# A first unit written out in one order, with unsplit second weights and more idle products

## The chip, the cores and the metric

The kernel runs on one core of a Trainium2 chip. The metric is the device time of one execution in microseconds (us): 1182.4 us, the median of 3 runs of the kernel before (1181.29 to 1183.06). A difference under 0.2% (2.4 us) cannot be told from no change here.

## The reference

Three blocks follow one another, on 8 batches. All inputs are random; the weights arrive as 8-byte floats and are rounded to 4-byte floats on the chip.

```python
# block 1: 8 batches, 8 heads, 512 tokens and 32 states of 64 numbers
scores = 1/8 * x @ state.T;  a  = softmax(scores)      # tokens read the states
scores2 = 1/8 * state @ x.T; a2 = softmax(scores2)     # states read the tokens
y = concat([a @ state, a2 @ x])                        # (8, 544, 512)
# block 2
xn = (y - mean) / sqrt(var + 1e-6) * g_ln
x2 = y + relu(xn @ w_ch1) @ w_ch2                      # w_ch1 512x2048, w_ch2 2048x512
# block 3
h = relu(x2 @ w_in);  c = conv over 3 neighbouring tokens of h
out = (h * sigmoid(c)) @ w_out                         # w_in 512x1024, w_out 1024x512
```

## The kernel before

**Units.** Block 2 is worked in nine units: units 0 to 7 are the 512 tokens of a batch, unit 8 (`NB`) the 256 state rows of all batches. In a unit the 2048 hidden numbers come in 16 pieces (m = 0 to 15) of 128. `L1(u, m)` makes piece m in a PSUM bank (`ph`), `relu_parts` brings it to SBUF, and `L2(u, m)` multiplies it with rows m of the second weights and adds into four PSUM banks (`acc`). `L1(u, m+1)` is always issued before `L2(u, m)`.

**Split numbers.** A 4-byte number is split into a rounded high part and the rest (`hH` and `hL`; weights `w[:, 0]` and `w[:, 1]`), both of the kind fp32r. `three` (lines 618 to 621) makes a product out of three matmuls: high by high, high by rest, rest by high. A product of two unsplit fp32 tiles (`L609`, `L647`) is one matmul of the program, and the trace shows two for it.

**Block 1 beside block 2.** While unit u is multiplied, generators (`token_norm(u)`, `attend(u+1)`) issue the norm of this batch and the attention of the next in small steps, one at each `gap(m)`. The tokens are not read out before `L1`: `z_tiles` multiplies the states of a batch with a quarter j of the first weights (`Z[u, j]`), and `L1` multiplies the attention weights (`AH`, `AL`) with that.

**Weights.** `Converter` rounds a raw 8-byte piece in steps: `round_1` (two ScalarE operations, L199, L200), `round_2` (two VectorE operations, L205, L206, and a GpSimd addition, L207), and for the second weights `third` (ScalarE L239, GpSimd L240), the split. There are 32 pieces: 16 of the first and 16 of the second weights. `z_first(j)` is unit 0's own step: it takes four rounded pieces of the first weights, makes their mean over the rows (L609), scales and shifts them on VectorE (L612), multiplies (L585), and stores them in DRAM (`w1d`, L615), from which all later units read them back through a ring of seven tiles (`pass_pairs`, L574). All DMAs are issued by SP, in order.

**What sets the order.** The first steps are written out by the string `START` (line 98, walked at line 777). From line 784 to the beginning of unit 1 a scheduler with a timeline of its own arranges the instructions (`need(2, m)` asks four pieces ahead; `tc.high_priority` in `gap`); from unit 1 on the order is as written. `warm` (line 766) issues products of a tile of zeros into a bank that nobody reads: 8 at the start and 2 in `START`.

**Names and lines.** PE is TensorE, DVE VectorE, ACT ScalarE, POOL GpSimd, SP SyncE. L361 reads tokens from states, L799, L290, L300, L325 are the states' attention of batch 0, L814 turns the convolution weights, L670 and L672 are `residual`.

Of the kernel before, what the change touches and what calls it, by code (L numbers as in the profile page):

```python
# [17 lines left out]
P = 128  # L18
# [24 lines left out]
def kernel(  # L43
# [29 lines left out]
    hH = new("hH", [2, S], F32R)  # L73
    hL = new("hL", [2, S], F32R)
# [14 lines left out]

    work = {**{c: f"b{c}" for c in "PQRUV"}, "s": "0"}  # L90
# [5 lines left out]

    WARM = 8
    START = "s0w1ws0a1bab01ca01cabcabc"
# [502 lines left out]
    def z_first(j):  # L601


        for q in range(KC):
            need(1, KC * j + q)
# [4 lines left out]
        for q in range(KC):  # L610
            t = w[q // 2][:, q % 2]
            V.scalar_tensor_tensor(t, t, gcol[:, q : q + 1], vp, op0=ALU.mult, op1=ALU.subtract)  # L612
        z_tiles(0, j, w)
        for g in range(2):
            nc.sync.dma_start(w1d[j, g], flat(w[g]))  # L615

# [11 lines left out]
    def hidden(m):  # L628
        return hH[:, m % 2], hL[:, m % 2]

    def relu_parts(m, p):
        h, l = (t[:, : p.shape[1]] for t in hidden(m))
        A.activation(h, p, AF.Relu)  # L633
        V.scalar_tensor_tensor(l, p, 0.0, f32(h), op0=ALU.max, op1=ALU.subtract)  # L634

    def L1(u, m):
# [13 lines left out]
        relu_parts(m, p)  # L650

    def L2(u, m, n):
        h, l = (t[:, :n] for t in hidden(m))
        for d in range(KC):
            c = slice(P * d, P * d + P)
            three(acc[d][:, :n], w2[m][:, 0, c], w2[m][:, 1, c], h, l, m == 0, m == M1 - 1)

    def residual(u, n):
# [10 lines left out]
        for d in range(KC):  # L669
            V.tensor_tensor(t[d], acc[d], rstd[u], op=ALU.mult)  # L670
        for d in range(KC):
# [4 lines left out]
    w2 = {}  # L676
# [13 lines left out]
    AHEAD = 4  # L690

    def need(a, m):
        i = place_of[a, m]
        conv_a.ensure(min(i + AHEAD, conv_a.total - 1))
        return conv_a.done[i]

# [8 lines left out]
    def whole(i):  # L705

        a, m = order[i]
        if a == 2:
            return None
        if m % 2 == 0:  # L710
            rounded.append(new(f"r{RAWS + m // 2 % 2}", [2, S]))
        if m + RAWS < M1:
            load_weight(place_of[1, m + RAWS])
# [7 lines left out]
    V.memset(f32(hL), 0.0)  # L721
# [44 lines left out]
    def warm(n):  # L766
        for _ in range(n):
            T.matmul(acc[3], hL[:, 1, :P], hL[:, 0], start=True, stop=True)

    warm(WARM)  # L770
    steps = {
        "s": state_start(),
        "0": tokens_start(0, x0T[0], sets[0]),
        "1": tokens_start(1, x0T[1], sets[1]),
    }
    conv_steps = {"a": conv_a.first, "b": conv_a.second, "c": conv_a.third}
    for c in START:
        if c == "w":
            warm(1)
        elif c in steps:  # L780
            next(steps[c], None)
        else:
            conv_steps[c]()
    tc_start.close()
    load_state(1)
    banks["free"] = pat

    round_1(craw, c0)
    round_2(craw, c0)

    def states_start():
        starts = [work, {"V": spare[5], "R": spare[6], "s": "1"}]
        E2Ts, z2s = [], []
        for g in range(2):
# [8 lines left out]
            E2 = new(starts[g]["R"], [S])  # L803
            z2s.append(state_weights(sc, E2, starts[g]))
            E2Ts.append(state_weights_t(E2, starts[g]))
        yield
        srs = [state_read(0, g, E2Ts[g]) for g in range(2)]
        srzs = [state_scale(g, srs[g], z2s[g], starts[g]) for g in range(2)]
        yield
        for g in range(2):  # L810
            state_store(0, g, srzs[g])
        yield
        cp = bank()
        T.transpose(cp[:, :24], c0[:, 0], ident[:24, :24])  # L814
        A.activation(cw, cp[:, :24], AF.Copy)

# [54 lines left out]
    units = [*range(NB - 1), NB, NB - 1]  # L871
    LAST = units[-1]
    for u, follow in zip(units, [*units[1:], None]):
# [11 lines left out]
        if u == 0:  # L885
            made += [(2, z_first, 1), (6, z_first, 2), (10, z_first, 3), (13, z_step, 1, 0)]
        elif u < NB:
            made += [(0, z_step, u, 1), (3, z_step, u, 2), (7, z_step, u, 3)]
            if u != LAST:
                made.append((10, z_step, LAST if follow == NB else follow, 0))  # L890

        def gap(m):
            if made and m >= made[0][0] and banks["held"] is None:
                _, make, *which = made.pop(0)
                make(*which)
            elif u == 0:
                with tc.high_priority(offset=100):
                    next(tasks, None)
# [196 lines left out]
```

## Time and profile before

| | |
|---|---|
| median of three runs | 1182.4 us |
| the profiled execution / its span | 1177.81 us / 1176.0 us |
| PE busy | 1125.9 us (96%) |
| DVE busy | 726.6 us (62%) |
| ACT / POOL busy | 444.2 / 207.8 us |
| chain that ended last: PE / DVE / ACT | 80% / 12% / 3% |
| granted PE clock, mean | 0.981 |
| read-back of first weights (`r<-w1d`): issue to landing | 4.5 us |

The span is what the trace shows between the first and the last instruction; the execution's own time has 1.8 us around it. A busy PE is not a PE at its peak: a matmul of 512 columns shows some 0.39 us of its own, but in a stream the next starts earlier, so the distance from start to start is the price of one.

### The profile page before, as it was taken

What the parts mean: (1) busy time and instruction counts of PE and PEld (TensorE: products, weight loads), DVE (VectorE), ACT (ScalarE), POOL (GpSimd) and SP (SyncE); (2) the same over time, 40 slices, a digit from 0 to 9 for tenths busy, and PEclk for the clock granted to TensorE, in tenths of its full rate; (3) what the DMA queues carried; (4) which work ended last, traced back from release to release, by engine and by line L of the source; (5) the groups of instructions that cost most, each with busy time, mean ns of one, the idle gap of its engine ahead of it and who ended that gap; (6) DMA issues with size and microseconds to landing.
All of it is one profiled execution on the core that took longest, in us unless ns stands there. A gap on an engine that the chain in (4) does not pass through costs nothing.

```text
span 1176.0 us, 14628 instructions
## 1 busy us (share of the span) xinstructions
PE 1125.9 (96%) x5459; PEld 863.8 (73%) x5459; DVE 726.6 (62%) x1134; ACT 444.2 (38%) x788; POOL 207.8 (18%) x314
## 2 busy tenths in 40 slices
PE   5698899999999999999989999999999999999997
PEld 4365567777777777777767888788788888888885
DVE  4899666566566475565665622577677666666553
ACT  5665333323233233233233222565344434334332
POOL 2565400000000000000000000265433312213110
PEclk8699999999999999999999999999999999999999
DMA  9643533432243333334314124322112102100001
GB/s 298 206 171 108 158 96 105 108 95 90 72 109 85 81 111 76 78 120 108 95 56 107 38 101 155 119 72 90 37 54 72 37 37 80 37 36 36 1 37 45
DMA packets 129283, 106.31 MB, mean 90 GB/s; under 512 B 103332, under 2 KB 107452, under 8 KB 128188
## 3 DMA queue, kind: packets, MB, share of 16 engines
q1 hardware_dynamic: 129212, 105.37, 29.6%
q8 instruction: 43, 0.70, 0.2%
q14 instruction: 28, 0.23, 0.1%
HBM read 83.85 MB, written 21.50 MB: 90 GB/s over the span
## 4 chain that ended last, share of the span: by engine, by line
PE 80%; DVE 12%; ACT 3%; issue 2%; POOL 2%; SPq 0%; DMA 0%; ACTq 0%; DVEq 0%; POOLq 0%
PE acc L619 14%; PE acc L620 14%; PE acc L621 14%; PE ph L619 7%; PE ph L620 7%; PE ph L621 7%; PE pat L585 2%; PE pat L621 2%; PE pat L619 2%; PE pat L620 2%; PE pat L361 2%; PE ph L647 2%; DVE tn L500 1%; ACT bQ L488 1%; DVE ctmp L206 1%
## 5 line engine op out<-in xcount | busy, mean ns | idle before, releaser
L619 PE MATMUL acc<-hH,w 128*128 128x512 f32 (+1 forms) x576 | 221.6, 395 | 2.2 <-ACT hH L633 2.2
L620 PE MATMUL acc<-hL,w 128*128 128x512 f32 (+1 forms) x576 | 220.4, 383 | 1.8 <-DVE hL L634 1.7
L621 PE MATMUL acc<-hH,w 128*128 128x512 f32 (+1 forms) x576 | 220.1, 382 | 0.0
L634 DVE SCALAR_TENSOR_TENSOR hL<-ph,hH 128x512 fp32r<-128x512 f32 (+1 forms) x144 | 94.2, 657 | 183.4 <-ACT hH L633 183.2
L633 ACT ACTIVATE hH<-ph 128x512 fp32r<-128x512 f32 (+1 forms) x144 | 81.6, 569 | 208.9 <-PE ph L621 171.3
L619 PEld LDWEIGHTS acc<-hH,w 128*128 128x128 f32 x576 | 108.1, 188 | 54.5 <-issue 15.9
L1008 DVE SCALAR_TENSOR_TENSOR w<-w,cw,w 128x544 f32<-128x544 f32 x128 | 109.9, 860 | 38.0 <-POOL w L1006 36.2
L620 PEld LDWEIGHTS acc<-hL,w 128*128 128x128 f32 x576 | 109.2, 190 | 24.3 <-DVE hL L634 4.2
L621 PEld LDWEIGHTS acc<-hH,w 128*128 128x128 f32 x576 | 109.0, 189 | 21.7
L207 POOL TENSOR_TENSOR ctmp<-ctmp,AH 128x512 int32<-128x512 int32 x1 | 1.3, 1304 | 610.7 <-DVE ctmp L206 610.7
L619 PE MATMUL ph<-AH,ZH 128*128 128x512 f32 x256 | 104.3, 408 | 0.7 <-ACT ZH L594 0.7
L620 PE MATMUL ph<-AL,ZH 128*128 128x512 f32 x256 | 100.9, 394 | 0.0
L621 PE MATMUL ph<-AH,ZL 128*128 128x512 f32 x256 | 100.1, 395 | 0.0
L989 ACT ACTIVATE w<-w 128x544 f32<-128x544 f32 x64 | 42.1, 657 | 129.4 <-DVE w L1008 129.4
L996 DVE TENSOR_TENSOR w<-w,w 128x512 fp32r<-128x512 f32 x64 | 49.5, 774 | 42.9 <-ACT w L995 42.1
L990 DVE TENSOR_TENSOR w<-w,w 128x544 f32<-128x544 f32 x64 | 48.8, 762 | 39.5 <-ACT w L989 39.5
L619 PEld LDWEIGHTS ph<-AH,ZH 128*128 128x128 f32 x256 | 48.5, 190 | 19.5 <-issue 6.6
L995 ACT ACTIVATE w<-w 128x512 fp32r<-128x512 f32 x64 | 40.4, 631 | 52.4 <-DVE w L990 47.4
L1006 POOL TENSOR_SCALAR w<-w,cw 128x544 f32<-128x544 f32 x64 | 47.7, 746 | 61.8 <-ACT w L1002 58.4
L621 PEld LDWEIGHTS ph<-AH,ZL 128*128 128x128 f32 x256 | 48.2, 189 | 11.8 <-issue 0.8
L620 PEld LDWEIGHTS ph<-AL,ZH 128*128 128x128 f32 x256 | 48.6, 190 | 9.7
L997 POOL COPY w<-w 128x32 f32<-128x32 f32 x64 | 17.5, 273 | 177.5 <-DVE w L990 177.5
(439 smaller groups left out, 2182.0 us busy)
## 6 DMA issues: line engine op xcount, KB each, us to landing
r<-w1d SPq DMA_DIRECT2D x64, 512.0 KB, 4.5
out_dram<-w SPq DMA_DIRECT2D x34, 256.0 KB, 2.2
w<-in_moe_w_ch_dram SPq DMA_DIRECT2D x16, 512.0 KB, 8.0
r<-in_moe_w_ch_dram SPq DMA_DIRECT2D x16, 512.0 KB, 4.9
x2d<-XT SPq DMA_DIRECT2D x8, 1024.0 KB, 4.9
bP<-in_x_dram SPq DMA_DIRECT2D x112, 64.0 KB, 2.5
bP<-in_x_dram SPq DMA_DIRECT2D x28, 256.0 KB, 3.8
w1d<-r SPq DMA_DIRECT2D x8, 512.0 KB, 2.6
```

The costliest lines, as they stand in the source:

```text
L361: T.matmul(xr[ql], s[:, 2 * g + ql], a, start=i == 0, stop=i == 2)
L619: T.matmul(o, lh, rh, start=first, stop=False)
L620: T.matmul(o, lh, rl, start=False, stop=False)
L621: T.matmul(o, ll, rh, start=False, stop=last)
L633: A.activation(h, p, AF.Relu)
L634: V.scalar_tensor_tensor(l, p, 0.0, f32(h), op0=ALU.max, op1=ALU.subtract)
L989: A.activation(c, c, AF.Sigmoid)
L990: V.tensor_tensor(c, c, h[:, 1 : SEQ + 1], op=ALU.mult)
L995: A.activation(g[:, 0], c[:, :S], AF.Copy)
L996: V.tensor_tensor(g[:, 1], c[:, :S], f32(g[:, 0]), op=ALU.subtract)
L1006: G.tensor_scalar(c, h[:, 0:SEQ], cw[:, f : f + 1], 0.0, op0=ALU.mult, op1=ALU.add)
L1008: V.scalar_tensor_tensor(c, h[:, k : k + SEQ], cw[:, k * FF + f : k * FF + f + 1], c, op0=ALU.mult, op1=ALU.add,)
```

## The change

Unit 0 is no longer arranged by the scheduler. Fourteen generators, one letter each, are stepped in the order of a string of 196 letters, up to the last step of unit 0. The second weights stay whole in unit 0: `L2(0, m)` multiplies the unsplit hidden piece with an unsplit weight, and `relu_parts` leaves the rest out there. The split of a second weight (now ACT L674 and DVE L675, none on POOL) comes later: six at the end of unit 0 (`SPLITS`), ten in unit 1 (behind `L2(1, 4)` to `L2(1, 13)`). Whole weights lie in pairs, and splits go to other places (`slot2`). The `w` letters stand for 24 zero products; the two of the old string are gone, the eight at the start stay. `residual` and `z_first` may stop halfway.

```diff
-    START = "s0w1ws0a1bab01ca01cabcabc"
+    START = "ss01abaa0b101aawwwwwwwwwwww0bwwww1SabaSbwwwwzbaLLzPbSawwwwPNSN..."
+    SPLITS = 6
...
     def relu_parts(u, m, p):
+        if u == 0:
+            A.activation(hid["H"][:, m % 2], p, AF.Relu)
+            return
+        if (u, m) == (1, 0):
+            hid["H"] = new("hH", [2, S], F32R)
...
     def L2(u, m, n):
...
-            three(acc[d][:, :n], w2[m][:, 0, c], w2[m][:, 1, c], h, l, m == 0, m == M1 - 1)
+            if u == 0:
+                T.matmul(acc[d], whole2[m][:, c], h, start=m == 0, stop=m == M1 - 1)
+            else:
+                three(acc[d][:, :n], w2[m][:, 0, c], w2[m][:, 1, c], h, l, m == 0, m == M1 - 1)
+
+    def split_w2(m):
+        w = w2[m] = new(slot2(m), [2, DM], F32R)
+        A.activation(w[:, 0], whole2[m], AF.Copy)
+        V.tensor_tensor(w[:, 1], whole2[m], f32(w[:, 0]), op=ALU.subtract)
...
+    streams = {
+        "s": (state_start(), acc),
+        "0": (tokens_start(0, x0T[0], sets[0]), acc),
+        "1": (tokens_start(1, x0T[1], sets[1]), acc),
+        "a": (firsts(), acc),
+        "b": (seconds(), acc),
+        "L": (reads_start(), acc),
+        "S": (states_start(), pat),
+        "z": (firsts_made(), pat),
+        "P": (products_start(), pat),
+        "T": (attend(1), pat),
+        "N": (token_norm(0), pat),
+        "d": (loads_start(), acc),
+        "c": (splits_start(), acc),
+        "w": (warm_steps(), acc),
+    }
...
+    for c in START:
+        banks["held"], banks["free"], banks["next"] = None, streams[c][1], turn.get(c, 0)
+        next(steps[c], None)
+        turn[c] = banks["next"]
...
+    splits = {(1, m): [m + 2] for m in range(SPLITS - 2, M1 - 2)}
```

PE's queue before, at the first `z_first` (`gmean` are the means' weights, `r` rounded first weights, `pat` and `ph` PSUM banks):

```order
L290 MATMUL pat_84<-ident_70,w_14_53_356 128x128 x4
L300 MATMUL pat_83<-XT_15_97,bV_350 64x128 x8
L300 MATMUL pat_84<-XT_15_97,w_13_56_366 64x128 x8
L325 MATMUL pat_83<-ident_70,bV_388 128x128
L325 MATMUL pat_84<-ident_70,w_13_60_394 128x128
L814 MATMUL pat_83<-ident_70,cbuf 128x24
L609 MATMUL pat_84<-r_40_245,gmean_73 128x512 x2
L609 MATMUL pat_84<-r_45_284,gmean_73 128x512 x2
L585 MATMUL pat_83<-r_40_245,sbd_36_189 32x512 x4
L585 MATMUL pat_84<-r_45_284,sbd_36_189 32x512 x4
L619 MATMUL ph_81<-AH_32_173,ZH_70_461 128x512
```

PE's queue in the changed kernel, at the same place (new line numbers: L612 is the old L609, L590 the old L585, L624 the old L619, L295 the old L290, L787 a zero product):

```order
L799 MATMUL pat_84<-w_10_34_175,sbd_36_189 64x256
L799 MATMUL pat_84<-w_11_35_176,sbd_36_189 64x256
L787 MATMUL acc_80<-hL_64 128x512 x4
L612 MATMUL pat_83<-r_38_217,gmean_73 128x512 x2
L612 MATMUL pat_83<-r_46_291,gmean_73 128x512 x2
...
L590 MATMUL pat_84<-r_38_217,sbd_36_189 32x512 x4
L590 MATMUL pat_83<-r_46_291,sbd_36_189 32x512 x4
L624 MATMUL ph_81<-AH_32_173,ZH_58_383 128x512
...
L295 MATMUL pat_83<-ident_70,bR_311 128x128 x4
L787 MATMUL acc_80<-hL_64 128x512 x4
```

The first first-layer product has moved ahead of the states' chain (L290, L300, L325 and L814 of before), and the 12 token reads (L361 of before), left out here, stand between the means and L590.

PE's queue before, one second-layer piece of unit 0, `L2(0, 2)` (`w_2` the split weight, `acc` the four banks):

```order
L619 MATMUL acc_77<-hH_63,w_2_65_425 128x512
L619 MATMUL acc_78<-hH_63,w_2_65_425 128x512
L619 MATMUL acc_79<-hH_63,w_2_65_425 128x512
L619 MATMUL acc_80<-hH_63,w_2_65_425 128x512
L620 MATMUL acc_77<-hL_64,w_2_65_425 128x512
L621 MATMUL acc_77<-hH_63,w_2_65_425 128x512
L620 MATMUL acc_78<-hL_64,w_2_65_425 128x512
L621 MATMUL acc_78<-hH_63,w_2_65_425 128x512
L620 MATMUL acc_79<-hL_64,w_2_65_425 128x512
L621 MATMUL acc_79<-hH_63,w_2_65_425 128x512
L620 MATMUL acc_80<-hL_64,w_2_65_425 128x512
L621 MATMUL acc_80<-hH_63,w_2_65_425 128x512
```

PE's queue in the changed kernel, the same layer at m = 2, and what follows it (`w_0` holds the pair of pieces 2 and 3):

```order
L667 MATMUL acc_77<-hH_63,w_0_60_398 128x512
L667 MATMUL acc_78<-hH_63,w_0_60_398 128x512
L667 MATMUL acc_79<-hH_63,w_0_60_398 128x512
L667 MATMUL acc_80<-hH_63,w_0_60_398 128x512
L590 MATMUL pat_83<-r_71_458,sbd_36_189 32x512 x4
L590 MATMUL pat_84<-r_78_532,sbd_36_189 32x512 x4
L624 MATMUL ph_81<-AH_32_173,ZH_89_600 128x512
L625 MATMUL ph_81<-AL_33_174,ZH_89_600 128x512
```

Twelve matmuls of the program have become four unsplit ones, and L590 is followed at once by the first-layer product that needs its result.

DVE's queue before, at the end of unit 0:

```order
L634 SCALAR_TENSOR_TENSOR hL_64<-ph_81,hH_63 128x512
L670 TENSOR_TENSOR tn_1282<-acc_77,rs_72_485 128x512
L670 TENSOR_TENSOR tn_1282<-acc_78,rs_72_485 128x512
L672 TENSOR_TENSOR XT_31_172<-XT_31_172,tn_1282 128x512 x2
L670 TENSOR_TENSOR tn_1282<-acc_79,rs_72_485 128x512
L670 TENSOR_TENSOR tn_1282<-acc_80,rs_72_485 128x512
L672 TENSOR_TENSOR XT_31_172<-XT_31_172,tn_1282 128x512 x2
L634 SCALAR_TENSOR_TENSOR hL_64<-ph_82,hH_63 128x512
```

DVE's queue in the changed kernel, there (L675 splits a second weight, L210 and L211 round the last piece, L689 and L692 are `residual`, L600 belongs to unit 1's first `z_step`):

```order
L675 TENSOR_TENSOR w_7_155_1041<-w_e_337,w_7_155_1041 128x512
L675 TENSOR_TENSOR w_8_156_1044<-w_e_337,w_8_156_1044 128x512
L675 TENSOR_TENSOR w_9_157_1047<-w_0_60_398,w_9_157_1047 128x512
L210 TENSOR_SCALAR ctmp_150_986<-ctmp_150_986 128x512
L211 SCALAR_TENSOR_TENSOR ctmp_150_986<-w_15_142_911,ctmp_150_986 128x512
L689 TENSOR_TENSOR tn_1072<-acc_77,rs_62_421 128x512
L689 TENSOR_TENSOR tn_1072<-acc_78,rs_62_421 128x512
L689 TENSOR_TENSOR tn_1072<-acc_79,rs_62_421 128x512
L689 TENSOR_TENSOR tn_1072<-acc_80,rs_62_421 128x512
L692 TENSOR_TENSOR XT_31_172<-XT_31_172,tn_1072 128x512 x4
L600 TENSOR_TENSOR ZL_167_1129<-pat_83,ZH_166_1128 128x512
L600 TENSOR_TENSOR ZL_167_1129<-pat_84,ZH_166_1128 128x512
```

Three splits and the last rounding now stand ahead of `residual`; three more splits follow the last row shown, and only then the rest (`hL`) of unit 1's first piece.

## Rows read from the trace of the kernel before

**Rows 1.** The page, part 2: busy tenths in 40 slices of the span.

```profile
PE   5698899999999999999989999999999999999997
DVE  4899666566566475565665622577677666666553
```

**Rows 2.** Windows: stretch, its length, busy us (instructions) per engine, PE clock, DMA.

```profile
15.00:134.00 119.00, 90.24 (x392) 59.60 (x392) 107.35 (x159) 71.68 (x127) 66.00 (x48) 0.84 0.61 191
134.00:172.90 38.90, 38.15 (x198) 24.78 (x196) 20.29 (x38) 10.38 (x20) 1.88 (x2) 1.00 0.32 96
172.90:255.50 82.60, 82.23 (x431) 60.98 (x424) 49.58 (x87) 26.82 (x47) 0.00 (x0) 1.00 0.35 96
```

**Rows 3.** Timeline of PE to the first first-layer product: start, us, instruction.

```profile
24.07 1.11 PE L456 MATMUL pat<-ident,bU 128*128 128x128 f32 x4 [7.47 <-DVE bU L450]
...
47.35 1.11 PE L290 MATMUL pat<-ident,w 128*128 128x128 f32 x4 [4.27 <-ACT w L284]
53.96 3.70 PE L609 MATMUL pat<-r,gmean 128*128 128x512 f32 x8
61.47 0.50 PE L619 MATMUL ph<-AH,ZH 128*128 128x512 f32 x1
```

**Rows 4.** Windows: the PE clock while PE waited for the first softmax.

```profile
20.00:24.00 4.00, 0.00 (x0) 0.00 (x0) 3.86 (x7) 2.71 (x5) 1.82 (x2) 0.50 1.02 399
```

**Rows 5.** Timelines of DVE (batch 0's states) and POOL (fourth rounded piece).

```profile
12.47 0.48 DVE L414 COPY sbd<-ph 128x128 f32<-128x128 f32 x2
...
31.94 1.62 POOL L207 TENSOR_TENSOR r<-ctmp,r 128x512 int32<-128x512 int32 x1 [1.02 <-ACT XT L363]
```

**Rows 6.** PE: unsplit matmuls (ns min/median/max; eight in the timeline); split ones, 12 apart.

```profile
L609 PE MATMUL pat<-r,gmean x32: 590/592/697, 54.0 to 137.6; 128*128 128x512 f32 x32
...
103.21 3.59 PE L609 MATMUL pat<-r,gmean 128*128 128x512 f32 x8
...
330.06 0.39 PE L619 MATMUL acc<-hH,w 128*128 128x512 f32 x1
...
332.78 0.39 PE L619 MATMUL ph<-AH,ZH 128*128 128x512 f32 x1
```

**Rows 7.** Lines, 15 to 135 us: instructions, count, busy us, mean ns, idle before.

```profile
L205 DVE TENSOR_SCALAR ctmp<-ctmp 128x512 int32<-128x512 int32 x22 | 14.8, 675 | 1.5 <-ACT ctmp L199 1.5
...
L206 DVE SCALAR_TENSOR_TENSOR ctmp<-w,ctmp 128x512 int32<-128x512 int32 x11 | 12.2, 1107 | 0.1
L634 DVE SCALAR_TENSOR_TENSOR hL<-ph,hH 128x512 fp32r<-128x512 f32 x12 | 8.1, 679 | 1.8 <-ACT hH L633 1.8
L612 DVE SCALAR_TENSOR_TENSOR r<-r,gcol,pat 128x512 f32<-128x512 f32 x12 | 8.1, 732 | 2.7 <-PE pat L609 2.7
```

**Rows 8.** Timeline of DVE: one piece rounded beside an idle POOL, then beside a busy one.

```profile
28.28 0.42 DVE L205 TENSOR_SCALAR XTt<-XTt 128x512 int32<-128x512 int32 x1
28.73 0.69 DVE L206 SCALAR_TENSOR_TENSOR XTt<-r,XTt 128x512 int32<-128x512 int32 x1
...
86.48 0.41 DVE L205 TENSOR_SCALAR ctmp<-ctmp 128x512 int32<-128x512 int32 x1
86.93 1.69 DVE L206 SCALAR_TENSOR_TENSOR ctmp<-r,ctmp 128x512 int32<-128x512 int32 x1
```

**Rows 9.** Lines, 15 to 135 us: POOL's part of the splits.

```profile
L240 POOL TENSOR_TENSOR w<-ctmp,w 128x512 fp32r<-128x512 f32 x11 | 15.2, 1392 | 1.5 <-ACT w L239 1.5
```

**Rows 10.** Waits, 30 to 175 us: us in total, times, longest.

```profile
POOL r L207 <- DMA w1d<-r: 17.9, 2, 9.2
```

**Rows 11.** Timeline of PE: a first-layer product behind `z_first`; unit 1's first second-layer product.

```profile
145.21 0.50 PE L619 MATMUL ph<-AH,ZH 128*128 128x512 f32 x1 [0.69 <-ACT ZH L594]
...
172.91 0.50 PE L619 MATMUL acc<-hH,w 128*128 128x512 f32 x1
```

**Rows 12.** Timeline of SP: eight loads of tokens, eight of states, as they were issued.

```profile
159.27 4.05 SPq L158 DMA_DIRECT2D bP<-in_x_dram  x8
...
35.59 4.62 SPq L141 DMA_DIRECT2D s_raw<-in_state_dram  x8
```

More of the change, by code (lines that the diff above doesn't have):

```diff
@@ L72 @@
     count = [0]
-    hH = new("hH", [2, S], F32R)
-    hL = new("hL", [2, S], F32R)
+    hid = {c: new(f"h{c}", [2, S], F32 if c == "H" else F32R) for c in "HL"}
     XT = {}
@@ L688, in load_weight @@
         )
[L690 to L695, printed above, removed]
     def temp(i):
@@ L767, in warm @@
         for _ in range(n):
-            T.matmul(acc[3], hL[:, 1, :P], hL[:, 0], start=True, stop=True)
+            T.matmul(acc[3], hid["L"][:, 1, :P], hid["L"][:, 0], start=True, stop=True)
     warm(WARM)
[L771 to L789, printed above, removed]
     def states_start():
         starts = [work, {"V": spare[5], "R": spare[6], "s": "1"}]
-        E2Ts, z2s = [], []
+        E2s, z2s, srzs = [], [], []
         for g in range(2):
@@ L815, in states_start, with reads_start, firsts, seconds @@
         A.activation(cw, cp[:, :24], AF.Copy)
+    def reads_start():
+        for g in range(2):
+            token_read(0, g)
+            yield
+    def firsts():
+        for _ in range(conv_a.total):
+            conv_a.first()
+            yield
+    def seconds():
+        for i, (a, m) in enumerate(order):
+            conv_a.second()
+            if a == 1 and m + RAWS < M1:
+                load_weight(place_of[1, m + RAWS])
+            yield
+    def firsts_made():
+        for j in range(KC):
+            yield from z_first(j)
+    def products_start():
+        L1(0, 0)
+        yield
+        for m in range(M1):
+            if m < M1 - 1:
+                L1(0, m + 1)
+                yield
+            L2(0, m, S)
+            yield
+        yield from residual(0, S)
+        z_step(1, 0)
+    def loads_start():
+        load_state(1)
+        yield
+        for m in range(LATE, M1):
+            load_weight(place_of[2, m])
+            yield
+        pass_pairs(RING)
+    def splits_start():
+        for m in range(SPLITS):
+            split_w2(m)
+            yield
+    def warm_steps():
+        while True:
+            warm(1)
+            yield
+    streams = {
[14 more added lines that the diff above has]
+    }
+    turn = {}
+    steps = {c: s[0] for c, s in streams.items()}
+    for c in START:
+        banks["held"], banks["free"], banks["next"] = None, streams[c][1], turn.get(c, 0)
+        next(steps[c], None)
+        turn[c] = banks["next"]
+    banks["free"], banks["held"] = pat, None
     x2, x2raw = {}, {}
@@ L930 @@
             gap(m)
-            if u == 0:
-                w2[m] = need(2, m)
             L2(u, m, n)
-            while u == 0 and made and made[0][0] < 12 and made[0][0] == m:
-                gap(m)
+            for k in splits.get((u, m), ()):
+                split_w2(k)
             if m == M1 - 1:
@@ L946 @@
                 gap(m)
-        residual(u, n)
+        for _ in residual(u, n):
+            pass
         if u != LAST:
```

80 lines of the change are left out of this document (35 added, 45 removed).

## The prediction

> **What bounds the kernel now.** I read the page's slices first: PE is busy for 80% or more of every slice from the third to the last but one, while DVE reaches 80% in slices two to four and nowhere else [rows 1]. Then the windows: from 15 to 134 us DVE works 107.4 of 119 us and PE 90.2, and the granted clock averages 0.84; from 134 to 172.9 PE works 38.2 of 38.9 us; and a unit after that takes 82.6 us of which PE fills 82.2 and DVE 49.6 [rows 2]. So the start and the larger half of unit 0 wait for VectorE and for the order of the queues; all that follows is PE alone. The change touches unit 0 and ten splits of unit 1, so nearly all of its worth must appear before the first second-layer product of unit 1, at 172.9 us [rows 11]. That moment is the anchor: I work out where it lies in the changed kernel, and what follows it stays as it is.
>
> **The early start, the gain.** Before, the first first-layer product begins at 61.5 us [rows 3]. Its means' products (L609) start at 54.0, though the last rounded piece that they need was finished at 31.9 + 1.6 = 33.6 us [rows 3, 5]: they stand in PE's queue behind the whole states' chain of batch 0 (L290 with a wait of 4.3 us, two rounds of L300, L325, L814). Now they stand ahead of it. Batch 0's states are ready on DVE at 12.9 us [rows 5]. From there to the fourth piece the new order gives DVE four pieces to round, 4 x 1.1 us beside an idle POOL [rows 8], eleven operations of the two softmaxes, the rests and a maximum of about 0.7 us each as L206 [rows 8], and some 1.2 us of small ones: 13.3 us; with 1 us of waits for the transposes between, DVE is done at 27.2. POOL's addition, 1.3 to 1.4 us like its other operations [rows 9], ends near 28.5 instead of 33.6 [rows 5]. From there: the last four matmuls of the means, 4 x 0.43 + 0.2 = 1.9 us, to 30.4; then the 3.8 us that lie before between the end of the means (54.0 + 3.7 = 57.7) and the first product (61.5) [rows 3]; and 0.8 us for four ACT copies of the token reads that now stand ahead of `Z`'s. That is 35.0 us, 26.5 us earlier. Bounds: no later than 61.5, no earlier than 33 (the copies and the wait at nothing). I take 35, the value next to the rows of the pieces.
>
> **The unsplit second layer, a cost on PE.** Eight matmuls of an unsplit product take 3.59 us, of which 0.59 is the last one's own time: 3.00 / 7 = 0.43 us each, and a product needs two, 0.857 us [rows 6]. A split product needs three, and twelve of a stream span 332.78 - 330.06 = 2.72 us: 0.227 each, 0.68 us a product [rows 6]. Unit 0 has 16 x 4 = 64 products, so PE gets 64 x (0.857 - 0.68) = 11.3 us more, not less. The unsplit form before has another operand in it (means' weights by `r`), so its price here is bounded: 0.43 us if the stream is dense as there, 0.59 if each runs alone; less than 0.43 no row shows. I take 0.43. The Trainium skill ("FP8 and Floating Point Precision", section "TensorE Precision Notes") says that true FP32 takes four passes through the array; at the 0.227 us of a split matmul this would be 0.91 us a product and 3.4 us more in all, as an estimate from that page. The trace has 0.857, and the sum goes by that.
>
> **What DVE, ACT and POOL lose.** The rests of the hidden pieces go: 16 x 0.68 us of DVE [rows 7]. The 16 splits leave POOL: 16 x 1.4 = 22 us [rows 9]. They come back on ACT and DVE at about 0.65 us each, six at the end of unit 0 and ten in unit 1. There DVE is busy 49.6 of 82.6 us [rows 2], and PE's work hides them; were it not to, ten would cost at most 6.5 us. POOL counts for more than its time, since a rounding step on DVE takes 0.69 us beside an idle POOL and 1.69 beside a busy one [rows 8]; the 22 L205 average 0.68 and L206 1.11 instead of 0.42 and 0.69 [rows 7, 8]. So a piece costs DVE between 1.1 and 2.1 us (0.41 + 1.69), with 1.78 the mean before. After the first product 26 pieces are left. The other VectorE work from there to `residual` is that of a later unit without its 16 rests and without `residual` (49.6 - 10.9 - 8 x 0.68 = 33.3), 12 scalings (8.1) and some 2 us left of batch 0, so 43.4 us [rows 2, 7]. DVE needs 43.4 + 26 x 1.1 = 72 to 43.4 + 26 x 2.1 = 98 us. By either end it is done (at 107 to 133 us) before PE.
>
> **PE from the first product to the anchor.** 16 + 2 first-layer pieces of 6 matmuls, 108 x 0.227 = 24.5 us. The second layer, 64 x 0.857 = 54.9. Three further means, 12 x 0.857 = 10.3. Attention, norm and `z_tiles`, as in a later unit: 82.6 less 288 x 0.227 = 65.4, so 17.2 [rows 2, 6]. The states' chain of batch 0, now behind the first product, at full clock: 4.1 (two rounds; L290 alone took 1.11 at half clock [rows 3]). One group of four idle products, 0.9; the other 20 (12, 4 and 4) stand where PE waits for the softmax (before, 7.5 us idle [rows 3]) and for the fourth piece, so they cost nothing; in front of a late result they would cost 0.23 us each, 4.6 at most. Sum: 111.9 us. Idle products are there for the clock: before, it was at half of 2.4 GHz after PE had idled [rows 4]; at half, the early products between 20 and 35 us would cost about 4 us more, which is in the range.
>
> **Waits of PE within.** Before, a first-layer product waits 0.7 us behind its `z_tiles` [rows 11]. In the new order, L590 is followed at once by that product for j = 1 to 3, and for j = 2 the means by L590 too: there PE waits for four scalings of 0.73 us [rows 7]. I count 1.3 + 2.3 + 0.5 us. A state transpose behind its softmax 0.5; at the end of the unit the first rest of unit 1 stands behind `residual` and three splits, 1.1. Sum 5.7, say 6. Waits that go: GpSimd no longer waits 17.9 us for `w1d` stores [rows 10], since those are now issued some 10 us before the tile is wanted again. SP is a single queue: its read-back of the first weights stands behind eight token loads that wait for PE and then 16 state loads, about 4.1 + 2 x 4.6 us [rows 12]. By this walk it lands 2 to 4 us ahead of its use, so I cost it at nothing; without that cover it is 1 to 5 us.
>
> **The sum.** 35.0 + 111.9 + 6 = 152.9 us for the anchor, against 172.9: 20 us less. The profiled execution of 1177.8 becomes 1157.8. The median of the timed runs lies 4.6 us above it, so I forecast 1162.5, written as 1163.
>
> **Rivals.**
> - *VectorE sets the pace after all.* Its pieces come in bursts, in order, and a PE step that needs one waits. DVE at 2.1 us a piece ends at 133, only 14 us before PE's last product, and every one of the three scalings can be late by a burst of some 3 us: anchor at 161, 1171. For it: DVE is full in this stretch before [rows 2]; against it: the POOL work that slowed it is a third less. The Trainium skill ("SBUF — State Buffer", section "Who interferes with whom") has it that the port pair which VectorE shares with GpSimd is an exclusive lock, so the loser waits for the whole instruction; the 1.69 us row agrees with that. By the rule at its fullest, 26 x 1.3 us on top of 72, DVE ends at 141, and this is why the case gets a fifth of the chance.
> - *The early start comes only in part.* If the fourth piece is as late as before (33.6) and the clock is at half until then, the first product starts near 44: anchor at 162, 1172. For it: DVE's order has both softmaxes around the pieces; against: POOL's fourth piece waited for ACT, not for a load [rows 5].
> - *No waits at all.* PE's work alone: anchor at 146 to 147, 1156. Against it: `z_tiles` waited before too [rows 11].
> - *Slower.* The unsplit products do not stream, because each needs its own weight load of 0.19 us in front: 0.43 + 0.19 = 0.62 us, 128 x 0.19 = 24.3 us on PE: 1187. It decides from 0.43 + 20 / 128 = 0.586 us a matmul. Against it: in the eight of rows 6 the loads are hidden.
> - *Not what it says.* That the order came out otherwise than the string is excluded by the queues themselves.
>
> **How the numbers follow.** Forecast (1159 to 1168) 0.55; VectorE 0.20; late start 0.09; no waits 0.11; slower 0.05. A range of 1154 to 1174 leaves out the slower case and the ends of the others. A difference under 0.2% is 2.4 us: only the slower case, or two of the middle ones together, come that near: faster 0.93, same 0.03, slower 0.04.
>
> **What would show it.** The first L624 into `ph` near 35 us; L667 two matmuls a product, 0.43 us apart; the first L624 into `acc` near 153; GpSimd with 32 additions and no split until block 3; a later unit still 82.6 us; the clock at 1.0 from 20 us on. Wrong would be: L624 after 45 us, L667 at 0.55 or more, waits of PE between 60 and 140 us of more than 12 us, or unit 1 longer than 85 us.

## The result and the profile after

The changed kernel takes 1165.1 us (median of four runs, 1163.6 to 1166.4) against 1181.9 for the kernel before (four runs beside it, 1177.7 to 1183.1): a ratio of 0.9864, with a 95% interval from 0.9836 to 0.9891. Forecast were 1163 and a range of 1154 to 1174. The profiled execution took 1165.58 us, 12.2 less than that of before (1177.81); the medians differ by 16.8. Both pairs are needed below, since the sum was made on profiled times. One of the six runs with four late weights (below) took 3932.5 us and is left out of its median.

The busy tenths of the changed kernel, to be read beside [rows 1]:

```profile
PE   8999999999999999999999999999999999999997
DVE  5888567565574665664765723577676666666563
```

PE is full from the second slice on, and DVE's nines are gone. The windows say the same by stage (length, busy us and instructions of PE, PEld, DVE, ACT, POOL, then clock, DMA share, GB/s): the start, the way from the first first-layer product to the anchor, and unit 1; compare [rows 2].

```profile
15.00:36.90 21.90, 20.88 (x97) 14.44 (x96) 17.70 (x34) 14.52 (x28) 7.02 (x6) 0.81 0.95 314
36.90:158.70 121.80, 116.68 (x454) 58.55 (x454) 96.31 (x154) 60.12 (x107) 35.91 (x28) 1.00 0.52 166
177.78:260.38 82.60, 81.90 (x419) 59.88 (x419) 54.07 (x94) 30.96 (x55) 0.00 (x0) 1.00 0.33 91
```

PE's timeline (start, us, instruction, idle before) with the places of [rows 3] and [rows 11]; L787 are idle products, L461 the transposes of the token weights, L612 the means, L624 the first of three split matmuls:

```profile
18.10 5.36 PE L787 MATMUL acc<-hL 128*128 128x512 f32 x12
23.29 0.60 PE L461 MATMUL pat<-ident,bU 128*128 128x128 f32 x4
23.65 1.17 PE L787 MATMUL acc<-hL 128*128 128x512 f32 x4
24.66 0.60 PE L461 MATMUL ph<-ident,bR 128*128 128x128 f32 x4
...
28.72 3.67 PE L612 MATMUL pat<-r,gmean 128*128 128x512 f32 x8 [0.39 <-ACT bR L289]
...
36.90 0.50 PE L624 MATMUL ph<-AH,ZH 128*128 128x512 f32 x1 [0.63 <-ACT ZH L599]
...
158.70 0.50 PE L624 MATMUL acc<-hH,w 128*128 128x512 f32 x1
```

The first product starts at 36.9 instead of 61.5 and the anchor lies at 158.7 instead of 172.9 [rows 11]. Behind the anchor 2.0 us are lost again: unit 1, measured from norm to norm, takes 82.60 us against 81.47, and each later unit 0.1 to 0.2 more. The clock, by windows (it stood at half from 20 to 24 us in [rows 4] too):

```profile
18.00:22.00 4.00, 4.00 (x11) 3.22 (x11) 3.48 (x7) 2.17 (x4) 1.12 (x1) 0.50 1.02 414
22.00:24.00 2.00, 2.00 (x10) 1.54 (x9) 1.33 (x4) 0.79 (x3) 0.00 (x0) 0.70 1.04 416
24.00:28.00 4.00, 4.00 (x28) 2.74 (x26) 3.37 (x7) 1.33 (x3) 1.30 (x1) 1.00 1.10 346
```

From 24 us to the anchor, and on to 582 us, it is full. All that PE waits for from the first product to the anchor, by the view of waits (us in total, times, longest):

```profile
PE ph L624 <- ACT ZH L599: 1.6, 3, 0.7
PE pat L590 <- DVE r L615: 1.4, 3, 0.8
PE pat L330 <- DVE bV L320: 1.1, 2, 0.6
PE pat L612 <- POOL r L212: 0.7, 1, 0.7
PE pat L590 <- ACT XT L368: 0.5, 1, 0.5
PE pat L330 <- DVE w L320: 0.5, 1, 0.5
```

Before rounding these are 5.7 us, 0.6 of them ahead of the first product. None ends in a DMA, so the read-back behind SP's queue of [rows 12] is hidden, and GpSimd's 17.9 us of [rows 10] are gone. The groups that answer to [rows 6] (count, busy us, mean ns, idle before):

```profile
L667 PE MATMUL acc<-hH,w 128*128 128x512 f32 x112 | 50.4, 594 | 0.0
...
L590 PE MATMUL pat<-r,sbd 64*32 64x512 f32 x80 | 9.0, 601 | 1.8 <-DVE r L615 1.4 <-ACT XT L368 0.5
L667 PE MATMUL acc<-hH,w_e 128*128 128x512 f32 x16 | 7.2, 592 | 0.0
```

and one piece of the second layer in the timeline:

```profile
83.22 3.59 PE L667 MATMUL acc<-hH,w 128*128 128x512 f32 x8
```

Eight unsplit matmuls of the second layer take 3.59 us, to the digit what the means took, with no idle time before them: they stream.

### The profile page after: what moved, and what is told of

Its sections match the earlier page's. It is cut to its first block, busy times and chain, and to the rows that moved or that the text cites. A ratio compares the mean times of both kernels' runs of the same rounds, so it can differ in the third digit from the quotient of the medians.

```text
span 1163.8 us, 14569 instructions
## 1 busy us (share of the span) xinstructions
PE 1134.8 (98%) x5417; PEld 851.1 (73%) x5417; DVE 720.4 (62%) x1134; ACT 442.4 (38%) x788; POOL 182.3 (16%) x298
## 5 line engine op out<-in xcount | busy, mean ns | idle before, releaser
L644 DVE SCALAR_TENSOR_TENSOR hL<-ph,hH 128x512 fp32r<-128x512 f32 (+1 forms) x128 | 83.3, 654 | 171.8 <-ACT hH L643 171.4
L624 PE MATMUL acc<-hH,w 128*128 128x512 f32 (+1 forms) x480 | 189.0, 394 | 0.0
L626 PE MATMUL acc<-hH,w 128*128 128x512 f32 (+1 forms) x480 | 181.9, 379 | 0.0
L625 PE MATMUL acc<-hL,w 128*128 128x512 f32 (+1 forms) x480 | 181.8, 379 | 0.0
L643 ACT ACTIVATE hH<-ph 128x512 fp32r<-128x512 f32 (+1 forms) x128 | 72.7, 568 | 196.7 <-PE ph L626 159.3
L624 PEld LDWEIGHTS acc<-hH,w 128*128 128x128 f32 x480 | 90.3, 188 | 44.4 <-issue 15.2
L624 PE MATMUL ph<-AH,ZH 128*128 128x512 f32 x256 | 106.8, 417 | 1.6 <-ACT ZH L599 1.6
L626 PEld LDWEIGHTS acc<-hH,w 128*128 128x128 f32 x480 | 90.2, 188 | 18.2
L625 PEld LDWEIGHTS acc<-hL,w 128*128 128x128 f32 x480 | 90.3, 188 | 16.7 <-DVE hL L644 0.3
L624 PEld LDWEIGHTS ph<-AH,ZH 128*128 128x128 f32 x256 | 48.5, 189 | 22.9 <-issue 8.8
L667 PE MATMUL acc<-hH,w 128*128 128x512 f32 x112 | 50.4, 594 | 0.0
```

The source lines that it names most:

```text
L624: T.matmul(o, lh, rh, start=first, stop=False)
L625: T.matmul(o, lh, rl, start=False, stop=False)
L626: T.matmul(o, ll, rh, start=False, stop=last)
L667: T.matmul(acc[d], whole2[m][:, c], h, start=m == 0, stop=m == M1 - 1)
```

## The experiments

All start from the changed kernel. The loss or gain is told against its own repeated median, 1164.2. The rounds ran on four chips; the kernel before, run beside each, had medians of 1178.5 to 1180.0, so the ratios can be compared too.

| what is different | median us | ratio to before, 95% interval |
|---|---|---|
| nothing (repeated) | 1164.2 | 0.9867 [0.9845, 0.9889] |
| no idle products | 1164.9 | 0.9869 [0.9853, 0.9885] |
| 7 + 2 idle products instead of 12 + 4 | 1164.6 | 0.9867 [0.9851, 0.9883] |
| states of batch 0 first | 1178.3 | 0.9985 [0.9976, 0.9994] |
| split at once | 1208.3 | 1.0237 [1.0220, 1.0253] |
| split one step later | 1188.2 | 1.0072 [1.0052, 1.0092] |
| rests of hidden pieces alone | 1184.4 | 1.0044 [1.0028, 1.0060] |
| GpSimd's subtractions alone | 1169.1 | 0.9915 [0.9898, 0.9931] |
| four late weights split first | 1168.8 | 0.9901 [0.9879, 0.9922] |
| the same, splits set apart | 1169.9 | 0.9905 [0.9880, 0.9930] |
| eight late weights split first | 1176.0 | 0.9970 [0.9956, 0.9983] |
| PE's order at three places | 1168.7 | 0.9909 [0.9891, 0.9927] |

**The kernel once more.** 

> The changed kernel itself once more, beside the runs of this round, so that differences of 1 to 5 us can be read from runs on one chip. Expected: 1165 (1163.5 to 1166.5), first first-layer product at 36 to 37, anchor at 158 to 159.

 Measured: 1164.2 (1162.3 to 1167.0), first product at 36.96, anchor at 158.82.

**No idle products.**

```diff
-    START = "ss01abaa0b101aawwwwwwwwwwww0bwwww1SabaSbwwwwzbaLLzPbSawwwwPNSN...
+    START = "ss01abaa0b101aa0b1SabaSbzbaLLzPbSaPNSN...
```

> All 24 idle products of zeros in the start's order are left out; everything else is the changed kernel (1165.1). Theory 1: they pay by the clock. In the changed kernel the clock went from half to full at about 23 us, behind twelve of them; without them PE is idle for 3 to 5 us before the token weights' transposes, the clock stays at half until about 30 us, the means (eight at 0.43) and the token reads run at half: the first first-layer product at 38.5 to 40 instead of 36.9, the time 1167 to 1168.5. Theory 2: they cost more than they give. The twelve took 5.36 us at half clock and held the first transposes (ready at 21.6) until 23.3, the next four held the second ones (ready at 23.4) until 24.7; without them the fourth piece is 1.2 us earlier and the products begin at 35.5, the time 1163.5 to 1164.

 Measured: 1164.9. PE's timeline of this run:

```profile
20.80 1.11 PE L461 MATMUL pat<-ident,bU 128*128 128x128 f32 x4 [3.33 <-DVE bU L455]
22.61 1.11 PE L461 MATMUL ph<-ident,bR 128*128 128x128 f32 x4 [0.70 <-DVE bR L455]
...
35.77 0.50 PE L624 MATMUL ph<-AH,ZH 128*128 128x512 f32 x1 [0.63 <-ACT ZH L599]
```

The first product is 1.1 us earlier than in the changed kernel, and the clock is at half until 26 us instead of 23. The earlier start does not bear out theory 2: in seven traces with the changed kernel's order up to there (its own, that of the repetition and those of five versions below that differ only later) the first product starts between 35.28 and 37.35 us. In these the clock is back at full between 22.2 and 24.0, so its later rise here, by one trace, is theory 1's sign without theory 1's time. By the medians the 24 products are worth nothing that can be measured, either way.

**Fewer idle products.**

```diff
-    START = "...101aawwwwwwwwwwww0bwwww1S...
+    START = "...101aawwwwwww0bww1S...
```

> Of the 12 + 4 idle products around the token weights' transposes 7 + 2 are left; the other eight stay. By the trace of the changed kernel seven at half clock end near 21.3, before the transposes' input is ready (21.6). Theory 1: the transposes then start at 21.7 and 23.5, the rounded pieces on VectorE move up by about 1.2 us and the first product starts near 35.7: 1164, if the clock is at full by 25 us all the same. Rival: fewer products leave the clock at half for some us longer, which takes back what is won or more: first product at 37 to 38, 1165 to 1166.5.

 Measured: 1164.6, first product at 36.31, inside that spread. Like the run above it shows no difference in time, and it decides between its two cases no better.

**States first.** All seven later steps `S` are moved ahead of the first `z`.

```diff
-    START = "...1SabaSbwwwwzbaLLzPbSawwwwPNSNbaSbPSbaSPdSPSad...
+    START = "...1SabaSbSSSSSSSwwwwzbaLLzPbawwwwPNNbabPbaPdPad...
```

> Only the order is changed: all steps of batch 0's states (transposes, reads, stores, the conv weights) stand ahead of the first means again, as in the kernel before; the unsplit products and the idle ones stay. Theory: the place of the states' chain made the early start. Its second exponential ends near 32 us and the read and the stores follow, so the means stand in PE's queue until about 36 and the first product starts at 43 to 46 instead of 36.9; 3.4 us of that is work that is only moved ahead, so the anchor is 3 to 6 us later: 1168 to 1171. Rival: the chain fits into waits of PE that are there anyway (GpSimd's fourth piece at 30.2), the first product at 38 to 40 and the time within 1 us of the changed kernel's 1165.

 Measured: 1178.3, 14 us more: the theory's direction, at more than twice its size. In PE's timeline of this run the chain waits link by link (L305 is the states' read), and the clock, 0.70 from 32 to 36 us and 0.50 from 36 to 40, makes the means slow as well: 5.65 us for the eight that took 3.67.

```profile
33.28 1.71 PE L305 MATMUL pat<-XT,bV 128*64 128x128 f32 x16 [3.36 <-ACT bV L297]
...
43.12 5.65 PE L612 MATMUL pat<-r,gmean 128*128 128x512 f32 x8
...
53.28 0.50 PE L624 MATMUL ph<-AH,ZH 128*128 128x512 f32 x1 [0.56 <-ACT ZH L599]
```

The first product is 16.3 us later; the stretch to the anchor is 3.4 us shorter (the moved work); the anchor comes at 171.7, 13 us later.

**Split at once.**

```diff
+            conv_a.third()
+            if a == 2:
+                w2[m] = conv_a.done[i]
...
-            if u == 0:
-                T.matmul(acc[d], whole2[m][:, c], h, start=m == 0, stop=m == M1 - 1)
-            else:
-                three(...)
+            three(...)
```

> The order of the first unit stays, but its second weights are split right behind their rounding (ACT copy, GpSimd rest, as in the kernel before), the hidden pieces get their rests on VectorE again, the products are three split matmuls, and the ten splits of unit 1 and six at unit 0's end go. Theory 1 (VectorE and GpSimd are near their limit): PE's work to the anchor falls by 64 x (0.857 - 0.70) = 10 us, but VectorE, 96 us busy of 122 in the changed kernel, gets 16 rests of 0.68 us (11 us) and with 16 x 1.4 us more on GpSimd slower rounding steps (14 us at the gap of 1.0 us seen before between 0.69 and 1.69, if most of the 26 meet it): 113 to 121 us in a stretch of 112, so PE waits again: anchor at 155 to 162, time 1162 to 1169, waits of PE from the first product to the anchor of 10 to 20 us instead of 5. Rival (PE alone counts, VectorE has room): waits stay at 5 to 7 us, anchor near 149, unit 1 back at 81.6: 1154 to 1156.

 Measured: 1208.3. Both theories fall: VectorE was not full (11.6 of 20 us from 40 to 60). ACT's timeline and DVE's in this run show the queues:

```profile
36.43 0.63 ACT L244 ACTIVATE w<-XTt 128x512 fp32r<-128x512 f32 x1 [4.21 <-POOL XTt L212]
```

```profile
40.62 1.29 DVE L600 TENSOR_TENSOR ZL<-pat,ZH 128x512 fp32r<-128x512 f32 x2 [5.58 <-ACT ZH L599]
```

ACT's copy of a split (L244) stands 4.21 us in front of its queue for GpSimd's rounding; behind it stand the token reads and `Z`, and DVE idles 5.58 us for these. That is a flaw of where this version puts its splits, so it was run again with the splits elsewhere.

**Split one step later.**

```diff
+            while conv_a.n2 < conv_a.n1:
+                split_next()
             conv_a.second()
...
-        if i % 3 == 2:
+        if i % 5 == 2:
```

> As the split at once (three split matmuls in unit 0, splits by ACT and GpSimd, rests of the hidden pieces on VectorE), but each split is issued one rounding step later than its weight's, with five scratch tiles instead of three, so that ACT and VectorE have other work between. Theory (the loss of the split at once, 1208, was the queues: ACT's copy stood right behind a rounding that ends on GpSimd, and VectorE, only 60 to 70% busy there, waited for scratch tiles): most of it goes, anchor at 152 to 162, 1160 to 1169. Rival (the split in the stream itself does not fit, by the load of VectorE and GpSimd and their slowing one another): anchor later than 168, over 1175, with VectorE over 85% busy from 40 to 150 us.

 Measured: 1188.2. Most of the excess went, as the theory said, but 24 us stay, which is the rival's time without the rival's sign: VectorE is busy for 86 of the 110 us from 40 to 150, 78% and not 85. In the 148 us from the first product to the anchor (183.0) PE's waits sum to 29.1 us against 5.0 in the changed kernel, and the mean clock is 0.92. The rests of the hidden pieces (L639) are the row that neither theory had: DVE stands idle 21.7 us in front of them.

```profile
L639 DVE SCALAR_TENSOR_TENSOR hL<-ph,hH 128x512 fp32r<-128x512 f32 x18 | 12.3, 685 | 21.7 <-ACT hH L638 21.7
```

**The rests alone.** The products stay unsplit; only the rests are made again.

```diff
-            A.activation(hid["H"][:, m % 2], p, AF.Relu)
+            h, l = (t[:, : p.shape[1]] for t in hidden(m))
+            A.activation(h, p, AF.Relu)
+            V.scalar_tensor_tensor(l, p, 0.0, h, op0=ALU.max, op1=ALU.subtract)
             return
```

> The changed kernel with one thing added back: VectorE makes the rest of each of unit 0's 16 hidden pieces again (0.69 us each), which no product reads; products stay unsplit, and what is computed stays the same. Theory (VectorE's queue): a rest stands behind its product and its ReLU, so VectorE waits 1 to 2 us for it ahead of softmax and roundings that PE needs next; with four such rests PE's wait for the state's transpose went from 0.48 to 3.45 us. Sixteen put 10 to 18 us of waits and of half clock on PE: 1175 to 1183. Rival (load only): 11 us more fit into the 25 us that VectorE has free between the first product and the anchor: 1165 to 1167, and then the loss of the later splits (1188) comes from the splits on ACT and GpSimd.

 Measured: 1184.4, 20.1 us more for 16 operations of 0.69 us. The answer for their line, and then the timelines of PE, DVE and GpSimd in this run at one of the places:

```profile
L640 DVE SCALAR_TENSOR_TENSOR hL<-ph,hH x16: 650/692/692, 37.9 to 161.9; 128x512 fp32r<-128x512 f32 x16
its engine sat idle before it (us, times) until:
  ACT hH L639: 19.5, 10
```

```profile
124.39 2.74 PE L612 MATMUL pat<-r,gmean 128*128 128x512 f32 x6
131.31 2.08 PE L612 MATMUL pat<-r,gmean 128*128 128x512 f32 x2 [4.18 <-POOL r L212]
```

```profile
119.25 0.69 DVE L640 SCALAR_TENSOR_TENSOR hL<-ph,hH 128x512 fp32r<-128x512 f32 x1 [2.68 <-ACT hH L639]
...
128.10 0.69 DVE L640 SCALAR_TENSOR_TENSOR hL<-ph,hH 128x512 fp32r<-128x512 f32 x1 [1.18 <-ACT hH L639]
...
129.16 0.69 DVE L211 SCALAR_TENSOR_TENSOR ctmp<-r,ctmp 128x512 int32<-128x512 int32 x1
```

```profile
129.99 1.28 POOL L212 TENSOR_TENSOR r<-ctmp,r 128x512 int32<-128x512 int32 x1 [5.33 <-DVE ctmp L211]
```

A rest can start only when PE has made the piece and ACT its ReLU; until then it holds DVE's queue, 19.5 us in ten places. Behind it stand the roundings: here the rest at 128.10 waits 1.18 us and stands ahead of the rounding (L211) whose piece GpSimd finishes at 131.27. PE waits 4.18 us for that piece, the fourth of the means, and from 132 to 136 us runs at a clock of 0.50. Some 1.8 of the 4.18 us are this rest, its wait and its own time; the others, such as the one at 119.25, were not taken apart. From the first product (35.28) to the anchor (176.65) PE's waits sum to 17.8 us against 5.0, and the mean clock is 0.95. The theory holds, a little above the upper end of its numbers.

Two things limit the figure. The four idle products behind the first product read the tile that the rests write, against what was expected of it; that wait of PE, 0.98 us, belongs to this version alone. And the kernel before has such rests too, but DVE stands idle only 8.5 us in front of 18 of them, in four places: so the 20.1 us are to be read as the price of rests in this order, not of rests as such. The same rests set later in VectorE's queue were not run.

**GpSimd's part alone.**

```diff
             conv_a.second()
+            if a == 2:
+                t = f32(i32(conv_a.tmp[i]))
+                G.tensor_tensor(t, whole2[m].rearrange(...), t, op=ALU.subtract)
```

> The changed kernel with another thing added back: behind each rounding of the 16 second weights GpSimd makes one more subtraction of the same size (the rest of a split, into the scratch tile, which nobody reads); the products stay unsplit, no ACT copies, no rests of hidden pieces. Theory: a rounding step beside a busy GpSimd takes 1.65 to 1.69 us instead of 0.69, so 16 x 1.3 us more of GpSimd slow perhaps 8 to 16 of VectorE's operations by up to 1 us, and pieces come later by GpSimd's 1.3 us each: 1167 to 1173. Rival: GpSimd is idle for 86 of 122 us, its operation falls beside ACT's and PE's work, and VectorE is in no hurry there: within 1.5 us of 1164.5.

 Measured: 1169.1, 4.9 us more, inside the theory's range. GpSimd goes from 35.9 to 56.0 us busy in the window from 36.9 to 158.7, and PE's waits up to the anchor from 5.7 to 9.9 us, at a clock of 1.00. The first half of the theory is hardly in it: the 26 rounding steps (L211) together took 26.0 us instead of 24.3. What makes PE wait was not taken apart further.

**Four late weights split ahead of their product.**

```diff
+    EARLY = 12
+    SPLITS = [*range(EARLY, M1), *range(4)]
...
-            if u == 0:
+            if u == 0 and m < EARLY:
```

> Of the six splits at the first unit's end four are made ahead of their product (second weights 12 to 15), whose 16 products are then three split matmuls each, with the rest of the hidden piece on VectorE; weights 0 to 3 are split at the end, 4 to 11 in unit 1. Theory: VectorE has room late in unit 0 (40.7 of 58.7 us busy from 100 to 158.7), so PE wins 16 x (0.857 - 0.70) = 2.5 us less about 0.5 of waits: 1162.5 to 1163.5 against the changed kernel's 1165. Rival: the products there are close behind their weights, and every split put in front adds a wait of 0.5 to 1 us: same or up to 2 us slower.

 Measured: 1168.8, 4.6 us more: the rival's direction, at more than twice its size. One wait of PE stands out, and the windows around it show the clock:

```profile
136.38 0.47 PE L331 MATMUL pat<-ident,bV 128*128 128x128 f32 x1 [3.46 <-DVE bV L321]
```

```profile
132.00:136.00 4.00, 0.93 (x4) 0.40 (x3) 3.83 (x6) 1.22 (x3) 2.62 (x2) 0.86 0.70 112
136.00:140.00 4.00, 3.62 (x9) 2.92 (x10) 3.32 (x7) 0.00 (x0) 0.48 (x1) 0.50 0.23 35
140.00:144.00 4.00, 4.00 (x15) 3.18 (x14) 0.00 (x0) 0.61 (x2) 0.81 (x1) 0.79 0.09 17
```

It does not carry all of the loss. The anchor is at 160.96, 2.3 us later than in the changed kernel; the profiled execution is 4.7 us longer. Part of the difference is a second wait, 1.30 us at 181.87 for VectorE's step of a norm in unit 1, where this edit starts the splits two steps earlier (whether that is its cause was not tested); around and behind it the clock was 0.83 and 0.74 in two windows of 4 us.

**The same, set apart.**

```diff
-    START = "...zPTPcTaabbTcPTPbPcPcPPPPTdPccccNTT"
+    START = "...zPTPcTaabbTPTPcbPPcPPcPPTdPccccNTT"
```

> Four late weights split ahead of their products as before, but the splits of 13, 14 and 15 are issued one to two PE steps later, behind the state's read and ahead of their product, so that ACT's copy does not stand in its queue for GpSimd's rounding. Theory A (in the run with four late ones the queue order was the price: ACT waited 1.87 us for GpSimd, PE 3.46 us for VectorE at the state's transpose, and then ran some 6 us at half clock): that wait falls under 1 us, the clock stays at full, unit 0 ends where the changed kernel's does or up to 2 us earlier: 1163 to 1166. Theory B (VectorE has no room late in unit 0, by its load): the wait moves to the late products, 2 to 4 us: 1167 to 1170.

 Measured: 1169.9. Theory A falls: ACT's wait for GpSimd shrank from 1.87 to 0.41 us, and PE's stayed at 3.45. Theory B has the time but not the place, since the wait did not move to the late products. DVE's timeline of this run shows what it was (the same softmax began at 126.38 in the repeated run of the changed kernel, straight behind `Z`):

```profile
125.47 1.29 DVE L601 TENSOR_TENSOR ZL<-pat,ZH 128x512 fp32r<-128x512 f32 x2 [1.20 <-ACT ZH L600]
128.07 0.69 DVE L647 SCALAR_TENSOR_TENSOR hL<-ph,w 128x512 fp32r<-128x512 f32 x1 [1.32 <-ACT w L646]
129.08 0.69 DVE L678 TENSOR_TENSOR w<-w,w 128x512 fp32r<-128x512 f32 x1 [0.31 <-ACT w L677]
129.69 0.68 DVE L345 TENSOR_REDUCE m<-bU 128x16 f32<-128x512 f32 x1
```

One rest (L647) and one split (L678) take 1.4 us, wait 1.6 for ACT, and stand ahead of the softmax, which is 3.3 us later; so is the scaled read that PE waits for. The six runs of this version spread with their mean clock: 1164.9 and 1165.1 at 0.995 and 0.993, the other four 1169.3 to 1171.1 at 0.987 to 0.990. So in the two runs where the clock held, the 2.5 us that PE was to win about paid for the longer wait, and the other 5 us go with the clock; only one of the slower four has a trace, so that this is the same wait in all is not shown.

**Eight late weights.** The same edit with `EARLY = 8` and `range(3)`. 

> As with four, but weights 8 to 15 are split ahead of their product (32 products in three split matmuls), 0 to 2 at the end, 3 to 7 in unit 1. Theory: twice as much, 32 x 0.157 = 5.0 us less 1 to 2 of waits, and unit 1 0.4 us shorter with five splits less: 1160.5 to 1162. Rival: VectorE gets 8 x 0.65 + 5 x 0.65 = 8.5 us more in the last 60 us of unit 0, between the roundings that the products wait for, and PE waits 3 to 6 us more: 1164 to 1167.

 Measured: 1176.0, 11.8 us more, beyond the rival. PE waits 6.16 us for GpSimd's piece at 126 us and 4.17 for the state's transpose at 146, and runs at half clock behind both.

**PE's order at three places.** One letter `P` of `START` moves as well.

```diff
+            late = m in (3, 7, 11)
-            if m < M1 - 1:
+            if m < M1 - 1 and not late:
                 L1(0, m + 1)
                 yield
             L2(0, m, S)
             yield
+            if late:
+                L1(0, m + 1)
+                yield
```

> From the changed kernel; only PE's order at three places of unit 0: second-layer product 3, 7 and 11 goes ahead of first-layer product 4, 8 and 12, which need a fresh `Z`, and the eighth stands between the means and the z products of the third pair. Theory: the 0.69 us ahead of the first-layer product at 125 us, the 0.84 and the stepping z products behind the third means (0.27 and some 0.8 that the modelled ends hide) go, since PE has 3.4 us of other work there: 1.5 to 2.5 us less, 1162 to 1163 against 1164.2 to 1165.1. Rival: VectorE is the later one at these places and the waits come back at the next step (the ReLU behind the delayed first-layer product, or the state's transposes): within 0.7 us of the changed kernel.

 Measured: 1168.7, 4.5 us more; the theory falls, and the rival put it too small. The waits aimed at behind the third means and at 125 us are gone, and these have come in PE's timeline:

```profile
97.26 0.66 PE L295 MATMUL pat<-ident,bR 128*128 128x128 f32 x4 [1.42 <-DVE ZL L600]
...
105.20 0.46 PE L330 MATMUL pat<-ident,bV 128*128 128x128 f32 x1 [3.28 <-DVE bV L320]
...
137.53 0.33 PE L330 MATMUL pat<-ident,bV 128*128 128x128 f32 x1 [2.11 <-DVE bV L320]
```

No version tried beats the changed kernel.

## Why the prediction came out right, step by step

- **The early start** was put at 35.0 and came at 36.9. The step that failed is "the other 20 cost nothing": twelve idle products at half clock (5.36 us) held the first transposes, whose input was ready at 21.6, until 23.3, and four more held the second, ready at 23.4, until 24.7. The fourth piece ended on GpSimd at 30.2 instead of 28.5 (33.6 before, [rows 5]). The clock was full from about 23 us and not from 20. What failed is the clock that the step took for granted. In the run of the rests alone, whose order up to there is the same, the clock stayed at full until 20.6 us; the twelve took 2.99 us and were done before the first transposes' input, the fourth piece ended at 28.6 and the first product came at 35.28, near the 35.0 that was worked out:

```profile
15.19 2.99 PE L789 MATMUL acc<-hL 128*128 128x512 f32 x12
20.42 0.96 PE L461 MATMUL pat<-ident,bU 128*128 128x128 f32 x4 [2.24 <-DVE bU L455]
...
35.28 0.50 PE L624 MATMUL ph<-AH,ZH 128*128 128x512 f32 x1 [0.62 <-ACT ZH L599]
```

- **The unsplit products** were sized exactly: 128 matmuls at 0.429 us from start to start are 54.9 us. The slower case, 0.62 each, is out.
- **PE's other work** was put at 57.0 us and took 61.8 (116.7 less 54.9). By distances from start to start, with the waits taken out, the first layer cost 27.6 and not 24.5 us: 0.256 a matmul, since a stream goes at 0.232 and a change of tile shape costs about 0.1. Attention, norm and z products cost 19.1 and not 17.2, because the stretch holds five groups of z products and a later unit four. The means and batch 0's states came to 14.1 instead of 14.4, and the four idle products to 1.0.
- **PE's waits** were put at 6 and sum to 5.0 from the first product on, most of them at the places named. The 1.1 us put at the end of the unit did not come; the state's transposes took 1.6 us and not 0.5, and 0.7 us for GpSimd's piece had not been named.
- **VectorE's need**, 72 to 98 us, is 96.3 by the trace. Of this 9.3 us are `residual`, four splits and two rests of unit 1, which the count left out; without them it is 87.0, in the middle, and a rounding step (L211, 26 of them) averages 0.93 us, between the 0.69 and 1.69 of [rows 8] and below the 1.11 of [rows 7]. PE did not fall behind it.
- **The anchor** was put at 152.9 and is at 158.7: 1.9 from the start, 4.8 from PE's work, less 1.0 of waits, which makes up the 5.8 us but for 0.1.
- **Behind the anchor** "what follows it stays as it is" failed by 2.0 us. About 1.0 is the ten splits of unit 1: in the two versions that split nothing there the unit takes 81.65 us. The 0.1 to 0.2 us in each later unit stay unexplained.
- **From profile to median** two errors met. The profiled gain is 12.2 instead of 20; but the 4.6 us by which the median of before lay above its profile are not there after, where median and profile agree within 0.5. Over the whole study the kernel before ran from 1177.3 to 1184.1, the changed one from 1162.3 to 1167.0. So the forecast of 1163 is nearer than its working: the gain was put at 20 us and is 12.2 by the profiles and 16.8 by the medians, and that the second error offset the first was luck.

The larger gap is in the reason. The prediction set down the 16 rests and 16 splits as time that VectorE and GpSimd lose beside PE's work, and the unsplit product as a cost to PE. Shown by the runs: putting the rests back costs 20.1 us, GpSimd's subtractions 4.9, and the whole split, though PE then has some 10 us less to do, 24. The rival that VectorE sets the pace was near the truth of the mechanism, but it counted busy time. What PE waits for is the order in VectorE's queue: a rest closes a loop from PE over ACT and VectorE back to PE, and VectorE, standing idle in that loop (19.5 us in the run of the rests alone), is late for what stands behind. The early order alone did not pay: with split weights it ran slower than before in both versions tried (1208.3 and 1188.2). The unsplit weights with the states first give 1178.3, 0.15% under before; unsplit weights in the scheduler's own old order were not run. By these runs the 16 us come from the two together. What the idle products add was tested only inside the new order, and there it is nothing that can be measured.

## What to carry to other kernels

An operation can cost its time and the wait in front of it, paid by all that stands behind it in the engine's queue: before pricing a removal by busy time, look at what the operation waits for and whom its queue serves. An engine with 20% idle time is not an engine with room, if that idle time is waiting in the middle of its queue. And when one part of a change adds work to the bounding engine, ask which loop through other engines it opens; against the split one step later, some 10 us more on PE took 34 us of waits and half clock away (24 by the time, 10 by PE's work).

## What was not expected of the hardware

- A wait of PE can cost more than itself. Behind a wait of 3.46 us the granted clock was 0.86, then 0.50, then 0.79 in three windows of 4 us; behind one of 4.18 us it was 0.50 for a window and 0.91 in the next. The waits of the changed kernel from its first product to the anchor, none over 0.84 us, left the clock at 1.00. But length alone does not tell: a wait of 2.54 us at 151 us in the run of the rests alone and one of 2.11 us at 138 us in the run with PE's order changed left it at 1.00 too, and behind one of 1.30 us (four late weights) it was 0.83 and 0.74.
- The same products met either clock at the start. In the changed kernel twelve products of zeros of 512 columns, 18.1 to 23.5 us, ran at half clock nearly to their end (0.50 from 18 to 22, 0.70 from 22 to 24), although PE had been busy without a break since 12 us; in the run of the rests alone, with the same order to there, they ran at full clock (1.00 from 12 to 18), and the first product came 1.6 us earlier.
- Between products of unlike tile shapes the distance from start to start grows: 0.523 us instead of 0.429 from an unsplit matmul to one with another tile, and 0.33 instead of 0.232 for the first split matmul behind such a tile.
